# Order of the opening stage of a delta-rule attention and feed-forward kernel: keys, scores, second inverse and weight conversion

## The chip, the cores and the metric

The kernel runs on one core of one Trainium2 chip. The metric is the device time of one execution in microseconds (us). A core has five engines that run side by side and wait for each other through semaphores: TensorE (PE) multiplies matrices, VectorE (DVE) and ScalarE (ACT) work element by element, GpSimd (POOL) does the same more slowly and issues transfers, and SyncE (SP) issues transfers. Each engine takes its instructions in the order in which the program gives them. Transfers (DMA) run on sixteen engines of their own.

## The reference

Four sequences (b) with eight heads (h) of 48 columns and 768 positions go through a delta-rule attention. Per head there is a 48 x 48 state. At each position t, with the key normalised to length one:

```python
y[t]  = q[t] @ state
v_old = k[t] @ state
state = state + beta[t] * outer(k[t], v[t] - v_old)
```

The outputs are laid side by side to 3072 tokens of 384 columns, x, and a feed-forward block follows, with g(h) = h / (1 + exp(-1.702 h)):

```python
out = g(x @ w_in) @ w_out        # w_in 384 x 2048, w_out 2048 x 384
```

The two weight matrices come as 64-bit floating-point numbers; q, k, v and beta are of 32 bits, and so is the output.

## The kernel before

**Units.** The 768 positions are cut into six chunks of 128. A unit is one chunk of one sequence with all its eight heads, so there are 24 units, numbered chunk by chunk: units 0 to 3 are the first chunk, 4 to 7 the second, and so on. Within a unit, 128 positions are four blocks of 32.

**What one unit needs.** Its keys are normalised (`normalize_mixed`: ACT squares, DVE sums to `ssq`, POOL takes the root to `rn`, DVE adds, inverts and scales KN). `turn` transposes the keys on TensorE (psT, copied by ACT to kT), and `gram` multiplies them with themselves (psG, copied by ACT to G). `prepare` does both and sends the diagonal 32 x 32 blocks of G through DRAM (Nd) to the tile NT, where the blocks of four units lie under each other. `invert(c)` inverts them on DVE, as multiplications (P) and sums (NT, YB), then sends the result (YS) through DRAM (Yd) to the tiles XB. For the first chunk this is done on the chip without DRAM. `scores` transposes the queries (psT, copied with the state to QS), multiplies them with the keys (psQ), subtracts the part for the state from V on DVE and copies the rest to M, which `select` masks on POOL.

**Hops.** With the inverse, a unit is solved block by block: `solve` multiplies XB with V (psU, copied by ACT to US), and `below` takes this out of the rows further down (psR, subtracted from V by DVE in `rest`). The first four units are solved in two pairs, units 0 and 1, then 2 and 3. `hops` yields eight hops for a pair; in each, one unit solves a block while the other is brought up to date below its last one. `put_out` then makes the outputs (psY) and the new state (ST). Through each hop the program weaves other work, in the order in which it is written: fills, keys, warm-ups and feeds.

**Fills.** `conversions` turns the 64-bit weights into 32-bit ones, piece by piece, w_in in nine pieces and w_out in fourteen. A piece takes five operations on DVE, and one on ACT (a rescaling with `low`); one call of `fill(1)` issues the next of them. When a piece is done, its raw place may be loaded again: `fetches` maps pieces to `fetch_in` (a quarter of w_in) and `fetch_out` (rows of w_out).

**Keys of units 4 to 8.** `keys` holds the generators of their preparation and takes one step of each at written moments (`begin`); `ahead_of(preparing, 1)` moves it by one moment.

**Warm-ups and feeds.** `warm(n)` issues n matmuls on constants, whose result nobody reads, so that TensorE stays active. `feed()` issues three matmuls of the first half of a feed-forward (`hidden`: ph, copied through the activation to gT by ACT); `ready_in` holds it back until its part of w_in is converted.

**Behind the hops.** Before, the program fills and feeds until w_in is done, then makes unit 4's scores, then runs the second inverse on DVE with a feed after each of its steps. `woven(n)` then takes the remaining units, three at a time in different phases; between its parts `spend` issues the second half of the feed-forward (`both_written` and `written`: po), which waits for w_out's pieces. From unit 4 on, TensorE's work is woven in this way until the end.

**Queues.** `sync` puts a transfer into SP's queue and `other_queue` into POOL's. Each queue issues in program order, and a transfer that waits holds back those behind it. Tiles come from rotating buffers, so a write may wait for the last reader of the buffer's former content.

The lines that the change touches are 315 to 328 (`normalize_mixed`), 940 to 948 (loads at the start), 969 (behind the first transposition of blocks), 1002 to 1022 (`keys`), 1024 to 1039 (first pair) and 1053 to 1100 (second pair and second inverse). Line 102 is a helper that keeps instructions in program order; most instructions are recorded under it.

## Time and profile before

| | before |
|---|---|
| median of three runs | 773.4 us (771.16 to 775.11) |
| the profiled execution | 773.04 us, of which its span 771.3 |
| TensorE busy | 751.0 us (97%) |
| VectorE busy | 440.6 us (57%) |
| ScalarE busy | 241.3 us (31%) |
| GpSimd busy | 128.4 us (17%) |
| mean granted TensorE clock | 0.973 |

The profile is of one execution. Busy times are sums over the instructions of an engine; matmuls overlap, so a busy TensorE isn't one at its peak. The granted clock is the share of full speed that TensorE was given. A chain, followed back from the last instruction to what released it, tells which engine carried the time at each moment; idle time of an engine that isn't in the chain costs nothing. Sorted by moment, the opening stage looks like this in the trace: the first inverse on DVE until about 43 us, the first pair's hops until 66, its outputs until 70, the second pair's hops until 95, its outputs until 101, the second inverse from 105.5 to 132.6, and w_out's conversion until 172.

### The profile page before, as it was taken

The numbers are of one execution on the slowest core, as the hardware profiler recorded it, in microseconds if no ns is written. First come the engines' busy times: TensorE is split into PE (matmuls) and PEld (weight loads), VectorE is DVE, ScalarE is ACT, GpSimd is POOL, SyncE is SP. The second block draws the span as 40 slices with busy tenths as digits, with TensorE's granted clock in tenths as the row PEclk, the third lists the DMA queues.
The fourth block names the chain that finished last, engine by engine and source line by source line (L and its number), as shares of the span: only waits on it lengthen the run. The fifth ranks groups of instructions, "written<-read, shape, count | busy, mean of one in ns | idle before, by whom it ended". The sixth has DMA issues, their size and how long they took to land.

```text
span 771.3 us, 19547 instructions
## 1 busy us (share of the span) xinstructions
PE 751.0 (97%) x8545; PEld 563.6 (73%) x8545; DVE 440.6 (57%) x896; ACT 241.3 (31%) x535; POOL 128.4 (17%) x134
## 2 busy tenths in 40 slices
PE   7889999889999999999999999999999999999998
PEld 6678788556687688678678678678678677687684
DVE  5997879896875565665665665665665621000000
ACT  4555632343333233233223223233223123121110
POOL 6133310011221221220221221231210000000000
PEclk8588999999999999999999999999999999999999
DMA  9976550644342142142142042042030020000000
GB/s 158 176 119 144 123 97 21 165 101 97 77 108 57 35 95 57 35 97 56 27 103 56 23 107 58 23 98 66 22 77 12 23 45 1 17 11 1 26 1 20
DMA packets 130661, 50.78 MB, mean 66 GB/s; under 512 B 105408, under 2 KB 126016, under 8 KB 130576
## 3 DMA queue, kind: packets, MB, share of 16 engines
q1 hardware_dynamic: 128112, 41.08, 24.9%
q0 software_dynamic: 2464, 8.46, 4.6%
q8 instruction: 67, 1.10, 0.6%
q14 instruction: 18, 0.15, 0.1%
HBM read 32.08 MB, written 16.25 MB: 63 GB/s over the span
## 4 chain that ended last, share of the span: by engine, by line
PE 81%; DVE 10%; SPq 4%; ACT 2%; DMA 1%; issue 1%; POOL 0%; DVEq 0%; ACTq 0%
PE po L102 30%; PE ph L102 27%; PE psY L102 6%; PE psU L102 5%; SPq L102 4%; PE psQ L102 3%; PE psG L102 3%; PE psR L102 3%; DVE w_out L102 2%; DVE P L102 2%; PE psT L102 2%; PE ps_warm L102 2%; DVE tmp L102 2%; DVE YB L102 1%; DVE NT L102 1%
## 5 line engine op out<-in xcount | busy, mean ns | idle before, releaser
L102 PE MATMUL po<-w_out,gT 128*128 128x384 f32 x768 | 265.2, 493 | 3.6 <-ACT gT L102 1.9
L102 PE MATMUL ph<-xT,w_in 128*128 128x256 f32 x1152 | 260.9, 383 | 0.3
L102 PEld LDWEIGHTS ph<-xT,w_in 128*128 128x128 f32 x1152 | 214.9, 190 | 32.6 <-issue 1.7
L102 PEld LDWEIGHTS po<-w_out,gT 128*128 128x128 f32 x768 | 141.3, 190 | 94.2 <-issue 3.1
L102 DVE TENSOR_TENSOR V<-V,psR 128x384 f32<-128x384 f32 (+2 forms) x72 | 40.1, 558 | 193.6 <-PE psR L102 193.1
L102 ACT ACTIVATE gT<-ph 128x512 f32<-128x512 f32 x96 | 56.4, 595 | 138.9 <-PE ph L102 138.8
L102 DVE TENSOR_TENSOR P<-NT,YB 64x8 f32<-64x8 f32 (+26 forms) x178 | 86.0, 483 | 4.9
L102 ACT COPY US<-psU 32x384 f32<-32x384 f32 x92 | 43.1, 469 | 138.8 <-PE psR L102 81.6
L102 PEld LDWEIGHTS psU<-V,XB 32*32 32x32 f32 x1536 | 60.1, 106 | 34.6 <-issue 27.6
L102 DVE TENSOR_REDUCE YB<-P 64x4 f32<-64x8 f32 (+27 forms) x178 | 77.2, 434 | 6.1
L102 PE MATMUL psU<-V,XB 32*32 32x48 f32 x1536 | 71.5, 205 | 0.6 <-DVE V L102 0.4
L102 PE MATMUL psR<-US,G 32*32 32x48 f32 x2576 | 64.2, 205 | 1.5 <-ACT US L102 1.5
L624 POOL TENSOR_SCALAR_AFFINE_SELECT M<-M 128x1024 f32<-128x1024 f32 x20 | 25.5, 1276 | 225.6 <-DVE M L102 166.8
L102 PEld LDWEIGHTS psR<-US,G 32*32 32x32 f32 x2576 | 54.6, 105 | 2.8 <-ACT US L102 1.6
L102 PE MATMUL psQ<-QS,kT 48*128 48x176 f32 (+1 forms) x384 | 37.6, 341 | 3.7 <-ACT QS L102 3.7
L102 DVE TENSOR_TENSOR P<-NT 64x256 f32<-64x256 f32 (+7 forms) x44 | 36.3, 826 | 0.5
L102 DVE TENSOR_REDUCE NT<-P 64x64 f32<-64x1024 f32 (+7 forms) x44 | 35.3, 803 | 1.5
L102 PEld LDWEIGHTS psQ<-QS,kT 48*128 48x128 f32 x384 | 31.1, 209 | 6.8 <-ACT QS L102 5.5
L102 PE MATMUL psG<-kT 48*128 48x128 f32 x384 | 32.8, 309 | 2.7 <-ACT kT L102 1.4
L102 PEld LDWEIGHTS psG<-kT 48*128 48x128 f32 x384 | 27.6, 208 | 5.9 <-ACT G L102 2.2
L102 ACT COPY o<-po 128x384 f32<-128x384 f32 x24 | 11.5, 477 | 61.7 <-issue 39.2
L102 ACT COPY M<-psQ 128x256 f32<-128x256 f32 x68 | 22.8, 377 | 23.4 <-DVE V L102 17.3
(100 smaller groups left out, 605.4 us busy)
## 6 DMA issues: line engine op xcount, KB each, us to landing
Nd<-G SPq DMA_DIRECT2D x16, 512.0 KB, 3.5
QP<-in_q_dram SPq DMA_DIRECT2D x24, 192.0 KB, 3.8
V<-in_v_dram SPq DMA_DIRECT2D x24, 192.0 KB, 3.2
out_dram<-o SPq DMA_DIRECT2D x24, 192.0 KB, 2.4
KN<-in_k_dram POOLq DMA_DIRECT2D x15, 192.0 KB, 3.7
NT<-Nd SPq DMA_DIRECT2D x20, 128.0 KB, 2.8
Yd<-YS SPq DMA_DIRECT2D x20, 128.0 KB, 2.5
XB<-Yd SPq DMA_DIRECT2D x20, 128.0 KB, 3.3
```

Source lines behind the costliest of these rows:

```text
L102: return lambda *a, **kw: tc.keep_in_program_order(op(*a, **kw))
L624: (pool if self.n < B else nc.gpsimd).affine_select(out=self.M, in_=self.M, compare_op=ALU.is_gt, fill=0.0, base=0, pattern=[[0, H], [1, 1 ...
```

## The change

- Keys of units 4 to 6 are loaded ahead of w_in's second quarter and of the values of units 2 and 3. The keys of unit 7 are loaded by SP into the tile `blocks`, as soon as its first content has been transposed; `normalize_mixed` takes them from there and writes the scaled keys to their usual place. Before, POOL's queue loaded them behind the first pair's outputs.
- `keys` runs at twice the pace in the first hops: two moments a hop from the first on. The five units begin at moments 0, 4, 8, 12 and 24 of 34, with one more moment between scaling and transposition.
- Fills in the first pair's hops are one and two in turn, in place of two. In the second pair's they are two in each hop. The scaling of V for units 2 and 3 moves by two hops.
- Warm-ups: from the fourth hop of the first pair on five in place of eleven; in the first three hops of the second pair five in place of eleven, and eleven in the fourth, where before a feed stood.
- Unit 4's queries are loaded before the hops and its values behind the first outputs; its scores are made in hops 3, 4 and 5 of the second pair (counted from 0). Feeds begin in hop 4 in place of 3.
- The second inverse follows the second pair's outputs at once, with 22 feeds in place of 19. Each half's feed-forward leaves its last block (`some(w, FC - 2)`) to the end, behind the inverse, since these need the last part of w_in.

```diff
-    def normalize_mixed(n):
+    def normalize_mixed(n, raw=None):
         K = KN[n % len(KN)][:, :, 0:D]
+        raw = K if raw is None else raw
...
-        act.activation(ksq, K, ACT.Square)
+        act.activation(ksq, raw, ACT.Square)
...
-        vec.tensor_tensor(K, K, rn.broadcast_to([128, H, D]), op=ALU.mult)
+        vec.tensor_tensor(K, raw, rn.broadcast_to([128, H, D]), op=ALU.mult)
...
-    for b in range(B):
+    for b in range(HB):
         load_values(b, sync)
-    fetch_in(1, other_queue)
-    D_ = spare("blocks").rearrange("p (b h k) -> p b h k", b=B, k=BS)
-    fetch_in(2, other_queue)
     for n in range(B, len(KN)):
         load(n, ((KN, k),), sync)
+    fetch_in(1, other_queue)
+    for b in range(HB, B):
+        load_values(b, sync)
+    blocks = spare("blocks")
+    D_ = blocks.rearrange("p (b h k) -> p b h k", b=B, k=BS)
+    fetch_in(2, other_queue)
...
+    seventh = blocks[:, 0 : H * D].rearrange("p (h d) -> p h d", h=H)
+    load(len(KN), (([seventh], k),), sync)
...
         def unit(n):
-            yield from normalize_mixed(n)
+            yield from normalize_mixed(n, seventh if n == len(KN) else None)
+            yield
             yield from prepare(n)
...
-        for t in range(24):
-            for u, begin in enumerate((0, 4, 7, 10, 13)):
+        for t in range(34):
+            for u, begin in enumerate((0, 4, 8, 12, 24)):
...
+    load(B, ((QP, q),), sync)
     preparing = keys()
     path = hops(*pair[:2])
     for i in range(2 * NB):
         together(*next(path))
-        fill(2 if i else 5)
-        if 2 <= i < 6:
-            values_scaled(pair[HB + (i - 2) // 2], range((i - 2) % 2 * NP, (i - 2) % 2 * NP + NP))
+        ahead_of(preparing, 1)
+        fill(1 + i % 2 if i else 5)
+        if 4 <= i < 8:
+            values_scaled(pair[HB + (i - 4) // 2], range(i % 2 * NP, i % 2 * NP + NP))
         if i in (3, 5):
             pair[HB + (i - 3) // 2].select()
-        if i > 0:
-            ahead_of(preparing, 1)
-        warm(NU)
+        warm(NU if i < 3 else NU // 2)
+        ahead_of(preparing, 1)
     for n, s in enumerate(pair[:2]):
         put_out(s, 2 - n)
-        load(len(KN) + n, ((KN, k),), other_queue)
+        if n == 0:
+            load_values(B, sync)
+        ahead_of(preparing, 1)
         fill(1 + n)
+    load(len(KN) + 1, ((KN, k),), other_queue)
...
-    ffn.append(hidden(xTs[0], gTs[0], slice(0, NTH), 1.3, True))
+    def some(work, n):
+        for _ in range(n):
+            yield next(work)
+
+    hiddens = [hidden(xTs[h], gTs[h], slice(0, NTH), 1.3, True) for h in range(HB)]
+    for w in hiddens:
+        ffn.append(some(w, FC - 2))
+    ffn += hiddens
+    first = new_step(B)
     path = hops(*pair[2:])
     for i in range(2 * NB):
         together(*next(path))
-        fill(2 if i < 5 else 3)
         ahead_of(preparing, 1)
-        if i > 2:
+        fill(2)
+        if i > 3:
             feed()
         else:
-            warm(NU)
+            warm(NU // 2 if i < 3 else NU)
         ahead_of(preparing, 1)
+        if i in (3, 4, 5):
+            next(first.scored, None)
         if 3 <= i < 6:
             fetch_out(i - 3)
-        if i == 5:
-            load(B, ((QP, q),), sync)
-            load_values(B, sync)
     for s in pair[2:]:
-        put_out(s, 2)
+        put_out(s, 1)
         feed()
-        fill(1)
-    ffn.append(hidden(xTs[1], gTs[1], slice(0, NTH), 1.3, True))
...
-    first = new_step(B)
-    next(first.scored)
-    t = 0
-    while not ("in", 3, 1) in done:
-        fill(2)
-        feed()
-        if t == 1:
-            run(first.scored)
-        ahead_of(preparing, 1)
-        t += 1
     run(preparing)
-    run(first.scored)
     inverting = invert(1)
-    for i in range(19):
+    for i in range(22):
         ahead_of(inverting, 1)
         feed()
     run(inverting)
     while ffn:
         feed()
-        fill(3)
+        fill(2)
```

## The prediction

> **What bounds the kernel now.** I read the page's chain first, then the same chain in order of time, then VectorE's (DVE's) timeline for its gaps, then TensorE (PE) in windows with its granted clock. Ax and Bx below are hop x of the first and of the second pair. The page's chain of work that ended last:

> ```profile
> PE 81%; DVE 10%; SPq 4%; ACT 2%; DMA 1%; issue 1%; POOL 0%; DVEq 0%; ACTq 0%
> ```

> The same chain in order of time, 100 to 180 us (start, length, engine, tile):

> ```profile
> 105.62 1.15 DVE NT L102
> 106.79 0.94 DVE P L102
> ...
> 131.38 1.23 DVE YS L102
> ...
> 144.71 1.68 POOL rn L102
> 146.41 0.18 DVE rn L102
> ```

> TensorE carries four fifths, but from the second inverse (105.54) until w_out is converted (172.4) DVE carries it. VectorE's timeline, three of its gaps (in brackets: idle before the line, and who ended it):

> ```profile
> 87.99 0.56 DVE L102 TENSOR_TENSOR V<-V,psR 32x384 f32<-32x384 f32 x1 [2.12 <-PE psR L102]
> 104.61 0.42 DVE L102 TENSOR_TENSOR V<-V,psQ 128x96 f32<-128x96 f32 x2 [2.49 <-PE psQ L102]
> 146.41 0.17 DVE L102 TENSOR_SCALAR rn<-rn 128x8 f32<-128x8 f32 x1 [1.78 <-POOL rn L102]
> ```

> From the first conversion (42.94) to the rn of unit 9 (146.41) there are eleven such gaps: 0.30, 0.82, 1.28, 1.03, 0.65, 0.22, 2.12, 0.55, 2.49, 0.18 before the inverse (9.64 us) and 1.78 behind it, 11.42 in all; the other 92.05 us are work. TensorE in windows of 3.41 us (busy, records, granted clock, DMA share, GB/s):

> ```profile
> 48.07:51.49 3.42, 3.42 (x109) 1.00 0.10 17
> 51.49:54.90 3.41, 1.96 (x58) 0.99 0.20 62
> 54.90:58.31 3.41, 3.41 (x43) 0.50 0.91 220
> 58.31:61.73 3.42, 3.42 (x43) 0.50 1.05 179
> 61.73:65.14 3.41, 3.41 (x26) 0.51 0.06 10
> 65.14:68.55 3.41, 3.41 (x55) 1.00 0.00 0
> ```

> Of these, the warm-up matmuls alone:

> ```profile
> 51.49:54.90 3.41, 0.96 (x10) 0.99 0.20 62
> 58.31:61.73 3.42, 2.07 (x11) 0.50 1.05 179
> 61.73:65.14 3.41, 2.40 (x11) 0.51 0.06 10
> ```

> The clock halves after a window with 0.96 us of dense work and comes back only after one with 2.40; 2.07 was not enough, though small solves filled the rest. TensorE's timeline shows what half clock costs:

> ```profile
> 16.49 2.56 PE L102 MATMUL psG<-kT 48*128 48x128 f32 x16 [0.28 <-ACT G L102]
> 57.73 2.52 PE L102 MATMUL ps_warm<-ident 128*128 128x256 bf16 x11
> 65.81 1.36 PE L102 MATMUL ps_warm<-ident 128*128 128x256 bf16 x11
> 78.51 1.16 PE L102 MATMUL psG<-kT 48*128 48x128 f32 x16
> ```

> [...] it switches at 41.2, 54.9 and 65.1, four and three windows apart. [...] the longest gap before 54.9 was 1.45 us, so I go by dense work per window. [...]

> **The change part by part.** From the rn of unit 9 on, DVE's order is the same in both kernels, and TensorE's from the last hidden matmul on. In front of that point DVE has the same operations in another order. So the profiled 773.04 us (span 771.3 and 1.74 around it; 0.4 below the median of 773.4) moves by the shift of this one point; only DVE's gaps can shift it, and the most to gain is 11.4 us.

> *Inverse earlier.* Behind it go the last multiplication of w_in's part (3,0), four operations of part (3,1) and five of w_out's first two pieces: 0.96 + (0.95+0.96+0.96+0.96) + (0.35+0.37+0.56+0.35+0.55) = 6.97 us. Work in front of the inverse falls from 105.54-42.94-9.64 = 52.96 to 46.0 us, so it starts at 88.9 plus the gaps. From its start to the rn of unit 9 there remain 92.05-46.0 = 46.05 us plus gaps g. Shift = start + 46.05 + g - 146.41 = start + g - 100.36.

> *g.* The 1.78 vanishes: ssq of unit 9 now stands 20 operations ahead of its rn. A new wait comes: ACT makes the last two gT (feed-forward block 14 of each half) ahead of two rescalings of w_out and of ksq of unit 9, and the gT need part (3,1). If that part ends at M, four feeds of 1.3 us end at M+5.2, gT 0.6, rescaling 0.6, ksq 0.5: M+7. DVE wants ssq at M+4.7 (10 operations of w_out, 2.3 us a piece). So g = 2.4; queued behind are all of w_out's conversions, and both_written waits for these. PE idles some 3 us before M at no price of its own (it has to wait for w_out later); if the clock halves there, add up to 1.7.

> *Keys early.* Three keys' loads, one by SP in place of POOL, and V of units 2 and 3 behind them: the three loads ended near 45 before, and values are needed from A4. I cost it at nothing; late keys would show as an ACT wait of up to some 2 us (0.63 at 78.1 now). The transposes and Grams of units 4 and 5 go into A4 to A7, their 8 Nd and 2 NT transfers with them; the last NT is issued near B4, over 10 us before the inverse wants it. On SP, V of unit 4 stands in front of the outputs' six xT transfers and waits only for A6.

> *Scores of unit 4 in B3 to B5.* They leave the serial stretch behind the hops: psT 0.45, ACT 0.86, psQ 1.51 and the 2.49 gap, about 4.2 us between the last ST (101.3) and the inverse (105.5). They cost B3 to B5 0.5 + 0.75 + 0.75 us of PE. Their M takes the buffer of unit 0, so fetch_out(2) waits on POOL for unit 2's outputs; behind it stand only fetch_out(3), which waits for w_in anyway, and unit 9. fetch_out(3) is now issued at M, lands about 4 us later and is wanted at M+8: hidden; without this cover, at most 4 us.

> *Half the warm-ups.* 37 of 121 in the hops go (A3 to A7 and B0 to B2: five in place of eleven, B3 eleven in place of a feed). At full clock PE per hop is 0.86 (solve and below) + psT 0.5 or psG 1.1 + 0.6 = 2.0 to 2.6 us, against DVE's 2.2 to 3.0 in A (V 0.56, ssq 0.55 or scaling 0.93, one or two fills of 0.7 to 1.0). But the dense work in the window from A3 to A4 is five warm-ups and perhaps a transpose, 0.6 to 1.1 us, where 0.96 lost the clock; and five warm-ups at half clock are 1.14 us of a hop, where a window with 2.07 did not bring it back. psG alone (3.14 us of the window from 13.94) did not either.

> At half clock the rows give solve and below 1.35, psT 1.11, psG 2.56, five warm-ups 1.14 (5/11 of 2.5). Outputs (1.37 at full clock) have no such row: between 1.37 and 2.2 times that, 3.0; I take 2.5. A5 starts at about 55.2 either way (DVE's sum puts V of A4 at 54.5). Then A5 5.05, A6 3.6, A7 5.0: 68.8. Outputs with psT 6.1: 74.9. B0 4.9, B1 3.6, B2 5.05: 88.5. B3 1.35 and eleven warm-ups 2.5: 92.4, where I let the clock return. Full clock then: psT 0.5, B4 3.0, B5 3.0: 98.8; DVE is late with scaling, two fills and psQ, so B7's solve is at 101.5; solve and feed to 103.6, two outputs and a feed 4.1: 107.7; ST 0.9: the inverse starts at 108.6. Shift = 108.6+2.4-100.36 = +10.6: 783.6 us.

> At full clock throughout: A7 ends at 63.1, outputs at 66.4, but ACT is then the brake (two G, four V scalings, kT, xT, rescaling: V of B1 at 73.9, where before has 74.74). B2's V at 76.1, B4 ends at 83.4, B5 at 86.4, B7's feed at 90.7, outputs 94.8, inverse near 96: -2.0 us.

> **The rivals.** *The clock holds* (not slower): psG and psT count as dense enough; the window 89.03 to 92.44 kept it with 1.16 of psG, 0.38 of ph and 0.25 of psT. 771 us; the walk's waits can be off by 3 either way, so 768 to 774. It decides from an inverse start below 98. *The outputs bring it back* near 75: from 74.9 B0 to B2 take about 7.2 in place of 13.6, B3 3.2; the inverse starts near 101.5, +3.5: 776.6. For it: 128-row matmuls[...]. *The clock does not return in B3 either*: B4 and B5 cost 2 us more each, 787.5. *Late data* (fetch_out(3) or a key): at most +4 on any of these. That the order doesn't change as said is excluded by the built order.

> **How the numbers follow.** Half clock through to B3 or beyond 55%; back at the outputs 22%; never lost 23%. The bound of 0.5% (about what a measurement here tells from no change) is 3.9 us: 769.5 to 777.3. Never lost splits into 13% same and 10% faster; back at the outputs 12% same, 10% slower; the rest slower, a few per cent of it returning early enough to be same: faster 0.10, same 0.28, slower 0.62. The range 769.8 to 788.5 takes in the late return; the likeliest's own is 778 to 788.

> **What would show it.** Right: PEclk 0.5 from about 55 to 90, psG of A and B at 2.5 us, gaps on DVE before V for psR of 1.5 to 3.5 us, inverse start near 108, a wait of DVE's ssq on ACT of about 2 us behind it. Wrong: clock 1.0 through the hops with the inverse before 98; or an NT or POOL transfer ending a DVE gap.

## The result

The changed kernel takes 776.5 us (median of 17 executions, 773.07 to 781.76), the kernel before beside it 772.84 (17, 770.62 to 775.11): a ratio of 1.0052, 95% interval 1.0033 to 1.0071. So it is about 3.7 us slower, where 783.6 was forecast. The profiled execution took 774.54 us, its span 772.8.

The page's chain answers to the one shown of before; nothing in it tells where time went:

```profile
PE 78%; DVE 11%; SPq 5%; DMA 2%; ACT 2%; issue 1%; DVEq 0%; ACTq 0%
```

The chain in order of time does. A stretch of the changed kernel, in the fourth hop of the second pair (B3):

```profile
78.61 0.04 PE psU L102
78.64 3.64 issue
82.28 0.29 PE psR L102 x2
```

In the middle of a run of 32 x 32 solves, whose data were all there, TensorE did nothing for 3.64 us. The word `issue` says that no semaphore, engine or transfer that the profile shows ended it. Before has no gap of this kind in its hops. VectorE's timeline behind the stall, at the inverse and up to rn:

```profile
82.85 0.56 DVE L102 TENSOR_TENSOR V<-V,psR 64x384 f32<-64x384 f32 x1 [4.97 <-PE psR L102]
87.52 0.56 DVE L102 TENSOR_TENSOR V<-V,psR 64x384 f32<-64x384 f32 x1 [3.06 <-PE psR L102]
89.75 0.42 DVE L102 TENSOR_TENSOR V<-V,psQ 128x96 f32<-128x96 f32 x2
90.59 0.56 DVE L102 TENSOR_TENSOR V<-V,psR 32x384 f32<-32x384 f32 x1 [0.42 <-PE psR L102]
103.22 1.23 DVE L102 TENSOR_TENSOR NT<-NT,bI 128x1024 f32<-128x1024 f32 x1 [0.18 <-issue]
104.48 0.17 DVE L102 TENSOR_TENSOR P<-NT,YB 128x4 f32<-128x4 f32 x1
107.41 0.95 DVE L102 SCALAR_TENSOR_TENSOR w_in<-tmp,w_in 128x768 f32<-128x768 f32 x1
137.23 0.56 DVE L102 SCALAR_TENSOR_TENSOR w_out<-raw,w_out 128x384 int32<-128x384 int32 x1 [0.56 <-ACT w_out L102]
140.23 0.55 DVE L102 TENSOR_REDUCE ssq<-ksq 128x8 f32<-128x384 f32 x1 [1.85 <-ACT ksq L102]
149.08 0.17 DVE L102 TENSOR_SCALAR rn<-rn 128x8 f32<-128x8 f32 x1
```

DVE pays for the stall with 4.97 us and then, at half clock, with 3.06. Of before's gaps, the 2.12 us at 87.99 are 0.42 here (90.59), and the 2.49 in front of the scores at 104.61 have no counterpart (89.75, no wait). So the inverse starts 2.3 us earlier than before (103.22 against 105.54) in spite of the stall. The wait in front of rn is gone and two on ACT have come, 0.56 and 1.85: 2.41 us. The granted clock of this execution changes at 42.80, 80.35 and 87.18 us, eleven and two times 3.413 us apart; in all eighteen profiles of this document, where there is more than one change between 38 and 200 us, they lie whole multiples of it apart, within 0.04. TensorE in windows of this length (busy, records, then the other engines; the last three columns are granted clock, DMA share and GB/s):

```profile
76.95:80.36 3.41, 1.69 (x51) 1.19 (x48) 0.89 (x2) 1.08 (x2) 0.00 (x0) 1.00 1.04 316
80.36:83.77 3.41, 1.49 (x14) 1.07 (x15) 0.89 (x2) 0.99 (x2) 0.00 (x0) 0.50 0.45 88
83.77:87.19 3.42, 3.42 (x57) 2.77 (x56) 0.69 (x2) 1.57 (x3) 0.00 (x0) 0.50 0.35 76
87.19:90.60 3.41, 3.41 (x62) 2.65 (x56) 2.48 (x7) 0.97 (x3) 1.85 (x1) 1.00 0.15 39
```

The stall cost the clock too: half from 80.4 to 87.2, not from 55 to 92 as forecast. Before that, all hops of the first pair ran at full clock.

The rn of unit 9 comes at 149.08 against 146.41, so 2.67 us later: the inverse starts 2.32 earlier and lasts 1.18 less (27.06 to 25.88), 5.54 us of work stand behind its end that stood ahead of its start, and the gaps grew by 0.63. The inverse is shorter although an operation of w_in stands in it (0.95, at 107.41). Its first multiplication takes 0.17 us, and 0.93 before; 0.93 is seen in the four profiles that have unit 4's scores right in front of the inverse and in no other, and why is not known. The rest I put down to the P buffers, two in number: before, an unfinished tmp of w_out held one of them all through the inverse. No run tried this alone, but with no tmp open (the last run below) the inverse lasts 25.15.

Behind rn this execution won 1.17. Before's lost the clock there from 170.9 to 174.3, and all profiles fit this: the stretch behind rn takes 623.7 to 624.3 us in the six that keep full clock from rn to the end of the conversions, and 624.9 to 626.3 in the twelve that have one or two windows of half clock between 141 and 180.

### The profile page after: what moved, and what is told of

Same layout as the page of the kernel before. It is cut to its first block, busy times and chain, and to the rows that moved or that the text cites. A ratio compares the mean times of both kernels' runs of the same rounds, so it can differ in the third digit from the quotient of the medians.

```text
span 772.8 us, 19475 instructions
## 1 busy us (share of the span) xinstructions
PE 744.2 (96%) x8508; PEld 558.7 (72%) x8508; DVE 439.0 (57%) x896; ACT 240.4 (31%) x535; POOL 129.0 (17%) x133
## 4 chain that ended last, share of the span: by engine, by line
PE 78%; DVE 11%; SPq 5%; DMA 2%; ACT 2%; issue 1%; DVEq 0%; ACTq 0%
PE po L102 30%; PE ph L102 27%; PE psY L102 6%; SPq L102 5%; PE psU L102 5%; PE psQ L102 3%; PE psR L102 2%; PE psG L102 2%; DVE w_out L102 2%; DVE P L102 2%; PE psT L102 2%; DVE tmp L102 2%; DVE YB L102 1%; DVE NT L102 1%; DVE w_in L102 1%
## 5 line engine op out<-in xcount | busy, mean ns | idle before, releaser
L102 PE MATMUL po<-w_out,gT 128*128 128x384 f32 x768 | 264.7, 493 | 5.3 <-DVE w_out L102 5.2
L102 PE MATMUL ph<-xT,w_in 128*128 128x256 f32 x1152 | 260.8, 383 | 1.4 <-DVE w_in L102 1.0
L102 PEld LDWEIGHTS ph<-xT,w_in 128*128 128x128 f32 x1152 | 215.3, 190 | 33.6 <-ACT gT L102 2.4
L102 PEld LDWEIGHTS po<-w_out,gT 128*128 128x128 f32 x768 | 141.0, 190 | 95.6 <-DVE w_out L102 7.6
L102 DVE TENSOR_TENSOR V<-V,psR 128x384 f32<-128x384 f32 (+2 forms) x72 | 40.1, 556 | 196.2 <-PE psR L102 195.6
L102 ACT ACTIVATE gT<-ph 128x512 f32<-128x512 f32 x96 | 56.5, 596 | 146.2 <-PE ph L102 146.1
L102 DVE TENSOR_TENSOR P<-NT,YB 64x8 f32<-64x8 f32 (+26 forms) x178 | 84.8, 476 | 4.7
L102 PEld LDWEIGHTS psU<-V,XB 32*32 32x32 f32 x1536 | 58.9, 105 | 37.1 <-issue 27.1
L102 ACT COPY US<-psU 32x384 f32<-32x384 f32 x92 | 43.2, 469 | 134.1 <-PE psR L102 79.1
L102 DVE TENSOR_REDUCE YB<-P 64x4 f32<-64x8 f32 (+27 forms) x178 | 77.2, 434 | 6.1
L102 PE MATMUL psU<-V,XB 32*32 32x48 f32 x1536 | 70.2, 204 | 3.4 <-DVE V L102 3.3
L102 PE MATMUL psR<-US,G 32*32 32x48 f32 x2576 | 63.1, 204 | 3.9 <-issue 3.6
L102 PEld LDWEIGHTS psR<-US,G 32*32 32x32 f32 x2576 | 53.6, 104 | 5.3 <-issue 4.3
L102 PE MATMUL psQ<-QS,kT 48*128 48x176 f32 (+1 forms) x384 | 37.9, 342 | 2.7 <-ACT QS L102 2.7
L102 DVE TENSOR_TENSOR P<-NT 64x256 f32<-64x256 f32 (+7 forms) x44 | 36.3, 824 | 0.3
L102 DVE TENSOR_REDUCE NT<-P 64x64 f32<-64x1024 f32 (+7 forms) x44 | 35.3, 803 | 1.5
L102 PEld LDWEIGHTS psQ<-QS,kT 48*128 48x128 f32 x384 | 31.1, 210 | 6.2 <-ACT QS L102 4.3
L102 PE MATMUL psG<-kT 48*128 48x128 f32 x384 | 33.0, 311 | 2.7 <-ACT kT L102 1.4
L102 PEld LDWEIGHTS psG<-kT 48*128 48x128 f32 x384 | 28.0, 210 | 5.3 <-ACT G L102 2.1
L102 ACT COPY o<-po 128x384 f32<-128x384 f32 x24 | 11.5, 477 | 61.7 <-issue 39.2
L102 ACT COPY M<-psQ 128x256 f32<-128x256 f32 x68 | 22.9, 376 | 23.8 <-DVE V L102 17.7
```

The source lines that it names most:

```text
L102: return lambda *a, **kw: tc.keep_in_program_order(op(*a, **kw))
```

## The experiments

**What holds TensorE up.** Four theories. F: TensorE's instructions come in pages through the DMA, and the page behind the gap is late because POOL issues 1.5 MB of w_out (rows 4 to 7) just ahead of it. C: fewer warm-ups lose the clock by themselves. A: the order of ACT's work. S: the stall belongs to this place of the program. For F speaks the DMA of the changed kernel from 70 to 90 us (busy share in tenths, half a microsecond each) and the queue of instructions in a window of 0.2 us from 79.2:

```profile
DMA  1396095899967899999889741001004644300810
q8 instruction: 1, 0.02, 46.6%
```

POOL issued the four from 71.3 to 73.8, and with what follows they fill the DMA engines from about 73 to 81. The one page, 16 KB, begins in this window only; 46.6% of sixteen engines for 0.2 us is 1.49 us, so it ends at about 80.8, and TensorE starts at 82.28. Over the execution this queue has 67 packets, 1.10 MB together, so 16 KB each; TensorE has 17,016 matmuls and weight loads together. That these packets are TensorE's pages is concluded from the counts.

The numbers of the instructions say the same. With its 147 control records TensorE has 17,163 instructions in the trace, or 67.04 times 256: 256 to a packet. In order of start, 2497 of them stand ahead of the stall. Of all eighteen profiles of this document, each gap over 0.18 us of TensorE between 44 and 110 us that ends by issue stands behind 1217, 2241, 2497 or 2753 instructions, whatever matmul comes next there: numbers that are multiples of 256 apart.

**Late rows** (the burst moved behind w_in's piece (2,2)):

```diff
-        ("in", 1, 1): lambda: (fetch_out(4), fetch_out(5), fetch_out(6), fetch_out(7)),
+        ("in", 2, 2): lambda: (fetch_out(4), fetch_out(5), fetch_out(6), fetch_out(7)),
```

> The changed kernel with one edit: w_out's rows 4 to 7 are fetched behind w_in's part (2,2) (about 95 us) in place of part (1,1) (about 71 us). Theory F: the 3.64 us in which TensorE stood still from 78.64 with no releaser, in the solves of B3, are its next page of instructions, late behind these four transfers of 384 KB; it also made the clock halve from 80.4 to 87.2. Then no such stall here, clock 1.0 through B3, inverse start near 97 to 98 in place of 103.2, time 4 to 6 us below the changed kernel: 771 to 773, even with before or slightly faster. Theory C (fewer warm-ups lose the clock by themselves): nothing changes, 776 to 777. Rival S (the stall belongs to this place of the program, whatever the transfers do): stall and time stay.

769.9 us against 772.52 of before, ratio 0.9979 (0.9966 to 0.9991). The DMA from 70 to 90 us, then the page (window of 0.2 us from 75.6), then TensorE's timeline at the same place of the program:

```profile
DMA  9999772111135304441006044440063967200000
q8 instruction: 1, 0.02, 35.4%
```

```profile
78.23 0.23 PE L102 MATMUL psR<-US,G 32*32 32x48 f32 x2 [0.20 <-issue]
```

POOL now issues the four after 93. The page begins 3.6 us earlier, and the stall is 0.20. Again TensorE starts 1.4 us behind its end. The clock is 1.0 through the hops, and the inverse starts at 96.93, 6.3 us earlier:

```profile
96.93 1.23 DVE L102 TENSOR_TENSOR NT<-NT,bI 128x1024 f32<-128x1024 f32 x1 [0.18 <-issue]
142.82 0.16 DVE L102 TENSOR_SCALAR rn<-rn 128x8 f32<-128x8 f32 x1
```

The moment of these four transfers was worth 6.6 us; S falls, and C as far as it has the stall. The kernel before with late rows alone was not run; its profile has no such stall that they could take away.

**All warm-ups** (eleven everywhere in the hops of the changed kernel, burst as it was):

```diff
-        warm(NU if i < 3 else NU // 2)
+        warm(NU)
...
-            warm(NU // 2 if i < 3 else NU)
+            warm(NU)
```

> The changed kernel with eleven warm-ups again wherever it has five. Theory C: the clock holds better and the time falls by 2 to 4 us, to 773 to 775. Theory F: TensorE gets 74 more instructions (48 of them in front of B3), so page borders shift; the hops are longer by 0.7 us each where TensorE is the brake (B0 to B2, some 2 us), the stall may fall elsewhere but the four transfers still meet a page: between 774 and 779, no clear gain.

770.6 us, ratio 0.9974 (0.9964 to 0.9984), below what either theory expected; inverse start 98.07. The stall is 0.56 us and falls among warm-ups, behind the same 2497 instructions. This alone doesn't tell the clock from the page: the edit adds 48 matmuls ahead of B3, which are 96 instructions (not the 74 expected), and the border between pages then stands at another place of the program.

**ACT's order** (four fills in place of two in the last loop):

```diff
     while ffn:
         feed()
-        fill(2)
+        fill(4)
```

> The changed kernel with four fills in place of two behind each of the last feeds, so that on ACT two more rescalings of w_out stand ahead of the last gT, and on DVE the ssq of unit 9 stands one piece of w_out later. Theory A: the waits of DVE on ACT behind the inverse (0.56 and 1.85 us) vanish and the time falls by 2.4 us, to about 774. If w_out's data or POOL's root end the wait in their place, it falls by less than 1.

776.59 us (8 executions, 773.08 to 782.48), as without the edit. But the wait is gone: ssq waits 0.36 in place of 1.85, w_out not at all, and from inverse to rn it takes 43.7 us in place of 45.9. The stall stayed (3.95 us), half clock follows from 82 to 92, and the inverse of this profile starts at 105.51; the effect on the time only shows once the stall is away (below).

**Few warm-ups in the kernel before**, nothing else:

```diff
-        warm(NU)
+        warm(NU if i < 3 else NU // 2)
...
-            warm(NU)
+            warm(NU // 2)
```

> The kernel before with the warm-ups of the change alone: five in place of eleven from A3 on and in B0 to B2. Theory C, and the prediction's main step: half clock through most of the hops, inverse start some 5 to 10 us later, time 778 to 783. Theory F: here the keys' transposes and Grams keep the clock as in the changed kernel; TensorE gets lighter in the hops, so the time is between 1 us faster and 2 us slower, unless a page of instructions meets the fetches of w_out.

777.27 us, ratio 1.0072 (1.0058 to 1.0086), and a stall came with it, at another instruction of TensorE's timeline:

```profile
77.91 0.23 PE L102 MATMUL psU<-V,XB 32*32 32x48 f32 x1 [3.26 <-issue]
```

So fewer warm-ups alone reproduce the loss, with half clock from 54 to 67 and from 78 to 88. Which of these costs, the next run tells.

**The same with late rows** (both edits in the kernel before):

> The kernel before with the changed kernel's warm-ups, which took 777.3 us with a stall of 3.26 us, now with rows 4 to 7 of w_out fetched at piece (2,2). If the stall is the burst's doing, it is gone; the half clock at 54 to 67, which lay ahead of the stall, stays, and that of 78 to 88 goes: 772 to 774.5 us. If fewer warm-ups lose the clock by themselves in both places, half clock is seen again after 78 and the time is 775.5 to 777.5.

772.08 us, ratio 0.9994 (0.9982 to 1.0007). The stall has shrunk from 3.26 us to 0.52, the half clock from 78 on is gone, and 5.2 us went with them. Half clock from 53 to 67 stays, 13.7 us of it, and costs nothing that can be measured against before, whose profile has 10.2 us of half clock in the same hops. So the loss of the warm-ups was the page's, not the clock's.

**The page's border moved** (the changed kernel, the 62 warm-ups of the prologue and the first two hops cut into 124 of half the columns):

```diff
-    def warm(n):
+    def warm(n, cuts=1):
...
+        w = 256 // cuts
         for _ in range(n):
-            pe.matmul(ps, lhsT=ones[:, 0:128], rhs=ones, start=True, stop=True)
+            for u in range(0, 256, w):
+                pe.matmul(ps[:, u : u + w], lhsT=ones[:, 0:128], rhs=ones[:, u : u + w], start=True, stop=True)
...
-    warm(NW)
+    warm(NW, 2)
...
-    warm(NY)
+    warm(NY, 2)
...
-        warm(NU if i < 3 else NU // 2)
+        warm(NU if i < 3 else NU // 2, 2 if i < 2 else 1)
```

> The changed kernel with 62 warm-ups of 256 columns ahead of the hops and in the first two hops issued as 124 of 128 columns: the same columns, 124 instructions more (matmul and weight load counted apart), about half a page of 256. The burst stays where it is. If an instruction page late behind the burst makes the stall, the border moves by half a page: one page is asked for before the burst and the next after it, so the 3.6 us in B3 vanish or shrink below 1.5 us, wherever they are, the clock stays 1.0 from 80 to 87, the inverse starts near 98 and the time is 769 to 772 us. If the stall belongs to that place of the program or to fewer warm-ups, it stays at B3 with 3 us or more, and so does the time, 776 to 777.

775.48 us, but from 769.92 to 781.53; the profile is of one of 770.29. TensorE's timeline has two small stalls in place of one:

```profile
76.61 0.27 PE L102 MATMUL psR<-U,G 32*32 32x48 f32 x2 [0.51 <-issue]
82.96 0.20 PE L102 MATMUL psR<-U,G 32*32 32x48 f32 x1 [1.07 <-issue]
```

The stalls stand behind 2497 and 2753 instructions: the numbers stay, and the places of the program that have them moved, as F says. The median missed F's number, so there is a second profile of this kernel:

> The changed kernel with its page border moved by half a page, once more: its executions reach from 769.9 us (clock 0.982) to 781.5 (0.959), and the profile at hand is of one of 770.3. If the slow ones are those where the stall comes back, the profile shows an issue stall of 3 us or more between 70 and 82. If they lose the clock in the hops by the way the windows fall, it shows half clock from about 55 without such a stall, 20 us or more of it.

776.77 us, clock 0.969: an issue stall of 2.06 that ends at 78.02, again behind 2497 instructions, and half clock from 62.7 to 66.1 and from 79.7 to 90. So neither theory alone: at the same border one execution has a stall of 0.51 and one of 2.06, and the second lost the clock ahead of it as well. How the other executions divide is not known.

**Where the clock's windows fall.** The changed kernel's executions spread as widely, and their times go with the mean clock: eight of 0.973 and above took 773.1 to 776.5 us, nine below 776.0 to 781.8. Three more profiles of it:

> The changed kernel once more, for the profile of another execution. The executions' times go with their mean granted clock (0.980: 773 to 774 us, 0.963: 781 to 782). If the stall is all there is, the half clock lies behind the stall again and is longer or shorter by whole windows of 3.4 us. If the hops with five warm-ups also lose the clock by themselves when the windows fall otherwise, an execution of 0.97 or below shows half clock from about 55 too, as the prediction had it.

> The changed kernel once more, for the profile of an execution with a clock of 0.971 or below. If the hops with five warm-ups lose the clock by themselves, such an execution shows half clock in the first pair's hops, between 53 and 75, ahead of the stall; if the stall is all there is, half clock lies behind it alone.

> As the run before, for another execution of the changed kernel: half clock between 53 and 75 if the hops lose it by themselves, behind the stall alone if not.

The first two took 775.06 and 774.02 us with stalls of 3.3 us and one window of half clock behind them (inverse start 101.95 and 102.16). The third took 778.39, clock 0.967. Its windows (columns as above):

```profile
50.33:53.74 3.41, 2.23 (x87) 1.78 (x78) 3.31 (x7) 0.47 (x1) 0.54 (x1) 1.00 0.02 5
53.74:57.15 3.41, 3.41 (x44) 2.62 (x44) 3.28 (x6) 3.32 (x9) 2.26 (x2) 0.50 0.42 117
57.15:60.57 3.42, 3.42 (x40) 2.60 (x39) 3.32 (x5) 2.27 (x7) 1.58 (x1) 0.50 1.03 206
60.57:63.98 3.41, 3.41 (x37) 2.63 (x33) 2.67 (x8) 1.99 (x5) 1.14 (x2) 0.50 1.00 179
63.98:67.39 3.41, 3.41 (x30) 2.90 (x29) 3.34 (x5) 2.46 (x8) 2.27 (x1) 0.50 0.05 10
67.39:70.81 3.42, 3.42 (x37) 2.90 (x35) 0.37 (x1) 1.74 (x7) 0.00 (x0) 0.50 0.35 70
70.81:74.22 3.41, 3.41 (x62) 3.12 (x64) 2.58 (x7) 2.50 (x8) 0.23 (x1) 1.00 0.31 65
```

This is the forecast half clock, from 53.7, in a part of the executions. The window that lost it held 0.72 us of warm-ups and 0.34 of psT; in the profile of the execution of 774.54 us the windows from 49.64 and 53.05 held 1.68 and 1.37 and kept it. The same program, cut elsewhere by the windows. It came back behind the outputs' psY (2.80 us in the window from 67.39). Five windows at half clock cost little: DVE was busy for 2.67 to 3.34 us of the first four, so TensorE's longer work lay beside it. The inverse starts at 104.82, 2.7 to 2.9 us behind the two other executions. The stall is there as well, 3.21 us at 84.56.

**Late rows with all warm-ups** (both edits above):

> Late rows as before and all eleven warm-ups in every hop. If the warm-ups count only by where they put the page border, the stall is absent here too and the 37 additional ones cost at most their own time on TensorE (about 0.09 us each, 3.4 us in all): inverse start 97 to 98.5, time 770 to 771.5, that is 0 to 1.5 us more than with five. If more warm-ups help by keeping the clock even without a stall, the inverse starts earlier than 96.9 and the time is below 769.5.

769.09 us (768.7 to 770.91), ratio 0.9962 (0.9948 to 0.9976), no stall in the hops. By rn the 48 more warm-ups (the expectation counted 37) cost 0.8 us (143.58 against 142.82); yet the median is not the 770 to 771.5 expected, nor above the 769.9 with five. No execution falls below a clock of 0.973, where seven of 22 did with five, and the slowest is 770.91 in place of 776.85.

**Late rows with ACT's order**, five warm-ups, and then with eleven:

> The changed kernel with w_out's rows 4 to 7 fetched at piece (2,2) and with four fills in place of two in the last loop, so that ACT issues its rescalings and ksq of unit 9 ahead of the last two gT. If the waits on ACT are worth their 2.4 us once nothing else is spread over them, ssq waits at most 0.4 us, the rn of unit 9 comes about 2 us earlier than the 142.8 of the run with late rows alone, and the time is about 767.9 us against 769.9. If another wait takes their place (TensorE idle for the delayed gT, w_out later), the rn stays at 142 to 143 and the time within 1 us of 769.9.

> The changed kernel with late rows, all eleven warm-ups in every hop and four fills in place of two in the last loop. If the removed wait on ACT (1.5 us of ssq's 1.85, 0.56 of w_out's) adds to the steady clock, the time is 767.0 to 768.0 us against 769.1 without the four fills, and no execution lies above 771. If the wait comes back elsewhere, it is 768.6 or more.

With five: rn at 140.64 in place of 142.82 and ssq's wait 0.35, both as expected; the median is not (769.18, 766.35 to 772.15; ratio 0.9961, 0.9948 to 0.9974), and above 770.5 are only executions with a clock of 0.968 or less. With eleven: 768.26 (766.64 to 769.18, 6 executions), ratio 0.9936 (0.9915 to 0.9957), rn at 141.01. So the wait on ACT is worth its 2.2 us at rn; less of it reaches the median.

**The parts that were meant to help**, each undone in the kernel with late rows. The scores behind the outputs:

```diff
-        if i in (3, 4, 5):
-            next(first.scored, None)
...
+    first = new_step(B)
+    run(first.scored)
     run(preparing)
     inverting = invert(1)
```

> The changed kernel with late rows (769.9 us) and unit 4's scores behind the second pair's outputs in one piece, as they stood before, in place of hops 3 to 5. By the prediction's step they then add a serial stretch of 4.2 us (psT, ACT's copy, psQ, DVE's wait for psQ) in front of the inverse and give TensorE back 2.0 us in B3 to B5: inverse start 99 to 101.2 in place of 96.9 and 772 to 774 us. If DVE is the limit of the hops and not TensorE, nothing comes back, and it is 774; if fills fill the stretch, the inverse starts below 98 and the time stays within 1 us of 769.9.

774.18 us, ratio 1.0034 (1.0016 to 1.0051): the scores in the hops are worth 4.3 us. The inverse starts at 99.13, 2.2 later, its first multiplication takes 0.93 in place of 0.17, and w_out waits 2.25 us for ACT in place of 0.56, another 1.7. VectorE's timeline has before's gap of 2.49 back, at 3.00:

```profile
97.94 0.42 DVE L102 TENSOR_TENSOR V<-V,psQ 128x96 f32<-128x96 f32 x2 [3.00 <-PE psQ L102]
```

The inverse behind w_in's last part, with five and with eleven warm-ups:

```diff
+    n = 22
+    while not ("in", 3, 1) in done:
+        fill(2)
+        feed()
+        n -= 1
     run(preparing)
     inverting = invert(1)
-    for i in range(22):
+    for i in range(n):
```

> The changed kernel with late rows (769.9 us), with three rounds of two fills and a feed in front of the second inverse, until w_in is done, and three feeds fewer in it: the inverse stands behind w_in's last part as before. The buffer of tmp is free during the inverse in both. If the order of DVE's work by itself is worth nothing and only its gaps move the rn of unit 9, the inverse starts some 5 us later, the two waits on ACT behind it (2.4 us) go or shrink, and the time is 767.5 to 770.5 us. If an early inverse has a worth of its own, the time is 772 or more.

> The changed kernel with late rows and all eleven warm-ups, and the second inverse behind w_in's last part. If five warm-ups were the cause of the half clock from 53 to 70, it is absent here in all executions and the clock stays at 0.973 or more. If the inverse's place by itself is worth nothing, the time is 767.5 to 769.5 us against 769.1 with the inverse in front; if an early inverse has a worth of its own, 771 or more.

With five 770.74 us, ratio 0.998 (0.9965 to 0.9996), from 767.81 to 773.03: its profile has half clock from 53.4 to 70.4 and no stall, ahead of all that the edit touches. With eleven 767.36 (767.08 to 769.24, 6 executions), ratio 0.9936 (0.9912 to 0.9959), the lowest median of all. VectorE's timeline:

```profile
101.94 1.22 DVE L102 TENSOR_TENSOR NT<-NT,bI 128x1024 f32<-128x1024 f32 x1
133.10 0.55 DVE L102 TENSOR_REDUCE ssq<-ksq 128x8 f32<-128x384 f32 x1 [1.49 <-ACT ksq L102]
141.96 0.16 DVE L102 TENSOR_SCALAR rn<-rn 128x8 f32<-128x8 f32 x1
```

The inverse starts 4.25 us later than with it in front (97.69), and rn of unit 9 comes 1.6 us earlier (143.58 there), 0.9 of it by the waits on ACT: an early inverse has no worth of its own. The medians even say that it costs some 1.7 us (769.09 with it), though the two ranges overlap.

## Why the prediction was right or wrong

**One point that sets the shift, the rn of unit 9: right, but not that only gaps can shift it.** Late rows move it by 6.3 us and the median by 6.6. Its sum of work from the inverse's start to rn was 2.6 us too high, 43.45 in place of 46.05 (149.08 - 103.22 - 2.41): by the formula the changed kernel's rn would have come 5.3 us later, and it came 2.67 later. Some 2.1 of this is the inverse, 1.18 shorter with 0.95 of other work in it; the rest may be that the sum adds full durations, while operations overlap at their ends (by 2.4 us in all between 103.22 and 149.08). The clock behind rn, worth 1 to 2 us, was left out as well.

**The gaps, 2.4 us: right**, 0.56 + 1.85 measured, and with four fills ssq's shrinks to 0.36. That the inverse's place as such gives nothing was the same step, and held.

**Scores, 4.2 us: right in size** (4.3), though only 2.2 of it lay in front of the inverse; the rest are the inverse's first multiplication and the wait on ACT, so the agreement is in part luck.

**Keys early, at nothing: not tested alone.** They end no wait of DVE in this profile, nor one of ACT's squares in the hops, where before waited 0.63 us for them.

**Half the warm-ups: the step that failed.** It let the clock fall at 55 and return in B3, at +10.6 us. Three terms of it were wrong. First, the count of dense work was too low, 0.6 to 1.1 us a window: where the windows fall well, they held 1.37 and 1.68 us of transposes and warm-ups, and the profile lost none there. Second, where it did fall (53.7), it came back with the outputs at 70.8, which was the second rival. Third, its price: 17 us at half clock moved the inverse by 2.7 to 2.9 us, and in the kernel before few warm-ups with late rows cost nothing; in the profile that lost the clock DVE filled the hops. The rival's 5.5 (101.5 against 96) was twice too much as well.

**What no step had: the late page.** 3.2 to 3.6 us of stall and one or two windows of half clock behind it put the inverse at 102 to 105, in all four profiles of the changed kernel. Taken away, the inverse starts at 96.93 and the time is 2.6 us below before's. That is near the rival "the clock holds" (inverse near 96, -2.0 us), though in part by luck: for an inverse at 96.93 its formula gives -1.0, rn came 3.6 earlier, and in the profile the half clock behind rn took 0.7 back. The forecast's sign was right for a reason that wasn't its own: this is luck. The 3.7 us are thus -2.6 of the change (769.9 against 772.5) and +6.6 of the stall with what follows (776.5 against 769.9); they miss 3.7 by 0.3 because each comparison has its own median of before. Both kernels' medians hold some executions with early half clock. With eleven warm-ups and late rows none of the three profiles loses it in the hops; what decides how many executions do so with five stays open.

## What to carry to other kernels

Look at gaps that end by "issue" and hold them against the DMA's share: a burst of transfers may delay the instructions themselves (a stall of 3.64 us here, 0.20 with the burst later), and adding or removing instructions ahead moves the place (96 more put it among warm-ups, behind the same 2497). Before a stage is paid with half clock, ask which engine fills it; and ask which phase of the clock's windows the profile happened to have. Ask of each piece of work that is moved earlier which gaps it takes away: the early inverse took away one of 1.78 us, brought two of 2.41, and gained nothing.
